# Linear attention and gated FFN on one core: k and v in 128 partitions with a padded tail slot, their loads at mid-group behind the q transpose, more dummy products at the start

## Chip, cores, metric

One core of a Trainium2 chip runs the whole program. The metric is the device time of one execution in microseconds (us). Single runs of one kernel scatter by 1 to 2% here, so medians and ratios over several runs are quoted. Engines are called as the profile calls them: PE is TensorE, DVE is VectorE, ACT is ScalarE, POOL is GpSimd, SP the queue that issues most DMAs.

## The reference

```python
# q, k, v: (8 batches, 8 heads, 576 rows, 64);  x below: 4608 rows of 512
kv  = einsum('bhsd,bhse->bhde', k, v)          # one 64x64 matrix per head
out = einsum('bhsd,bhde->bhse', q, kv)
out = out / sqrt(mean(out*out) + 1e-6) * g_norm
x   = out as (4608, 512)
xn  = x / sqrt(mean(x*x) + 1e-6) * rms_g
y   = (silu(xn @ w_gate) * (xn @ w_val)) @ w_out   # 512 -> 1536 -> 512
```

## The kernel before

The kernel works in nine groups of 512 rows: group n takes the first 512 rows of batch n, and the ninth group takes the 64 rows that are left of each batch. A group is 16 slots of PE work: 12 `up` slots (8 products of 512 columns each, into `g_ps` and `v_ps`) and 4 `down` slots (12 products each, into `o_ps`). Between the slots stand small steps that prepare the next group: k and v are loaded in float32 (`kraw`), cast to bf16 (`k_t`, `v_t`), multiplied to `kv_all`; q is loaded (`stage`), cast (`q_t`) and transposed by a DMA (`qt`); the attention output is scaled (`xna`) and transposed (`xnt`). In the timelines below each engine takes its instructions in program order (a silu stands behind two k casts that wait 1.22 us for their load), so where a step stands decides what waits behind it.

```python
def load_kv_parts(b, name, cuts):              # KP = 96 partitions, KT = 6 tokens each
    src = {"k": k, "v": v}[name][b].rearrange("h (p t) d -> p h (t d)", t=KT)
    st = kraw_pool.tile([KP, H, KT * D], FP32, name="kraw")
    ...
        yield nc.sync.dma_start(out=st[:, hs, :], in_=src[:, hs, :])
# ... (cut)
for n in range(1, B + 1):
    # ... (cut)
        nxt.qT_dma()                           # q of batch n+1, at the start of group n
    # ... (cut)
        if n == 1:                             # batch 3: load at slot 0, casts on POOL
            at(0, lambda: load_kv(3, "k"), lambda: load_kv(3, "v"))
            for i, piece in enumerate(pieces(3, "k", nc.gpsimd) + pieces(3, "v", nc.gpsimd)):
                at(3 + i, piece)
        at(1, lambda n=n: load_q(n + 2))
    if n + 3 < B:                              # k, v of batch n+3 late in the group
        at(11, lambda n=n: load_kv(n + 3, "k"), lambda n=n: load_kv(n + 3, "v"))
        # ... (cut)
    if 2 <= n < B - 2:                         # ... and cast early in the next, on ACT
        todo = pieces(n + 2, "k", nc.scalar)[2:] + pieces(n + 2, "v", nc.scalar)
        for slot, piece in zip((0, 1, 2, 3, 4, 9), todo):
            at(slot, piece)
    if n + 2 < B:
        at(10, kv_batch(n + 2, 0))             # the k/v products
        at(11, kv_batch(n + 2, 1))
```

## Time and profile before

| | before |
|---|---|
| median when the prediction was made | 363.52 us (3 runs, 360.28 to 364.48) |
| span of the profiled run | 358.4 us |
| PE busy | 324.1 us, 90% |
| first FFN product | 26.4 us |

The page's slices come first: 40 equal parts of the span, each digit a busy share in tenths; the PEclk row is the PE clock that the throttle granted.

```profile
PE   6569998999599899799978999799999999999994
...
PEclk9758999999899999999999999999999999999999
```

PE is full except at the start, at slice 11, and once about every four slices. At the start its clock is half. To see the periodic gap, the span is cut at the first FFN product of each group (the boundaries are read from the timeline). The columns are: stretch, length, busy time with count for PE, PEld, DVE, ACT, POOL, then granted clock, DMA share and GB/s. These are groups 1, 2, 4 and 6:

```profile
69.32:109.94 40.62, 36.44 (x207) 18.25 (x208) 22.58 (x45) 14.89 (x27) 12.15 (x16) 0.96 0.74 173
109.94:145.67 35.73, 33.60 (x184) 16.20 (x184) 19.21 (x42) 20.95 (x36) 0.00 (x0) 1.00 0.64 143
181.82:219.57 37.75, 33.60 (x184) 16.23 (x184) 19.21 (x42) 20.94 (x36) 0.00 (x0) 1.00 0.61 142
256.91:289.03 32.12, 32.07 (x161) 14.85 (x161) 18.54 (x40) 13.42 (x24) 0.00 (x0) 1.00 0.26 66
```

Group 6 loads no k and v any more and is PE-bound (32.07 of 32.12). Groups 1 to 5 lose 2 to 4 us each (length minus PE busy). The waits of PE (who waits, for whom, total us, times, longest) say for what:

```profile
PE g_ps L408 <- ACT silu L401: 8.9, 4, 3.4
PE att_ps L231 <- POOL v_t L101: 4.7, 4, 3.8
PE att_ps L275 <- DMA qt<-q_t: 3.5, 4, 1.6
```

Why ACT is late with silu is seen in its timeline at the start of group 2 (start, duration, instruction, and in brackets how long the engine stood idle before it and for what):

```profile
110.14 0.59 ACT L99 COPY o_sb<-o_ps 128x512 f32<-128x512 f32 x1 [2.00 <-PE o_ps L421]
111.95 1.57 ACT L99 CAST k_t<-kraw 96x768 bf16<-96x768 f32 x2 [1.22 <-DMA kraw<-in_k_dram]
113.43 0.59 ACT L401 ACTIVATE silu<-g_ps 128x512 bf16<-128x512 f32 x1
```

Two k casts stand in front of the group's first silu, and their load is still on its way. The queue that issued it, in its own timeline:

```profile
103.82 0.57 SPq L87 DMA_DIRECT2D kraw<-in_k_dram  x1
104.49 0.52 SPq L87 DMA_DIRECT2D kraw<-in_v_dram  x1
105.58 5.54 SPq L433 DMA_DIRECT2D out_dram<-o_sb  x2
111.21 9.16 SPq L258 DMA_TRANSPOSE qt<-q_t  x1
```

The q transpose is issued behind 2.36 MB of k and v and takes 9 us to issue. Over all seven of them, issue to landing:

```profile
DMA to landing us min/median/max: 4.4/11.4/13.5
```

At the start, stretches of PE (length, busy, clock, DMA share, GB/s):

```profile
10.00:13.00 3.00, 0.24 (x2) 1.00 1.09 240
13.00:15.00 2.00, 1.43 (x13) 0.53 1.09 252
15.00:29.00 14.00, 10.92 (x77) 0.50 1.04 374
```

After 2.8 us of idle the clock drops to half and stays there. While k and v come, the DMA engines are full (a share above 1: the records of their packets overlap) yet move only 240 GB/s; for the weights after 16 us it is about 380.

### The profile page before, as it was taken

The page shows a single profiled execution, that of the slowest core. Times are in us where ns is not written, and L with a number is a line of the kernel's source. Part 1 is how long each engine was busy: PE and PEld are TensorE (multiplying, and loading weights), DVE is VectorE, ACT ScalarE, POOL GpSimd, SP SyncE. Part 2 cuts the span into 40 slices and gives each one's busy share as a digit, 9 for nine tenths or more (in the row PEclk, how much of TensorE's full clock was granted, in tenths as well). Part 3 has the DMA queues.
Part 4 walks back from the last instruction along what each step waited for, and adds up shares of the span by engine and source line. Part 5 has one row for each costly group of instructions (what it writes and reads, how often), then busy time and mean ns, then how long its engine had stood idle before and what let it go on. Part 6 is the DMA issues. An engine that isn't in the chain of part 4 may idle for free.

```text
span 358.4 us, 4740 instructions
## 1 busy us (share of the span) xinstructions
PE 324.1 (90%) x1776; PEld 158.7 (44%) x1786; DVE 180.9 (50%) x392; ACT 170.4 (48%) x293; POOL 33.4 (9%) x48
## 2 busy tenths in 40 slices
PE   6569998999599899799978999799999999999994
PEld 2346354455244354345433454345444445444441
DVE  3552655547831396049604880379139625933310
ACT  3484336427136663476436822873346237423321
POOL 0023360543400000000000000020000000000000
PEclk9758999999899999999999999999999999999999
DMA  8999999959559903990399019990530260061013
GB/s 220 273 385 308 223 377 217 243 146 232 136 117 230 269 1 66 228 316 9 62 226 301 29 24 191 279 182 3 164 72 0 53 183 1 0 119 59 0 30 89
DMA packets 62114, 54.31 MB, mean 152 GB/s; under 512 B 34440, under 2 KB 54924, under 8 KB 62092
## 3 DMA queue, kind: packets, MB, share of 16 engines
q1 hardware_dynamic: 57952, 53.48, 60.3%
q0 software_dynamic: 4128, 0.52, 2.3%
q8 instruction: 14, 0.23, 0.3%
q14 instruction: 8, 0.07, 0.1%
q10 hardware_dynamic: 12, 0.00, 0.0%
HBM read 37.75 MB, written 9.44 MB: 132 GB/s over the span
## 4 chain that ended last, share of the span: by engine, by line
PE 54%; DMA 38%; POOL 3%; SPq 2%; issue 1%; ACT 1%; DVE 0%; POOLq 0%
PE o_ps L421 21%; DMA kraw<-in_v_dram 15%; PE g_ps L408 15%; PE v_ps L414 15%; DMA qt<-q_t 14%; DMA stage<-in_moe_w_gate_dram 5%; DMA kraw<-in_k_dram 2%; PE att_ps L275 2%; PE att_ps L231 2%; POOL v_t L101 2%; DMA stage<-in_q_dram 2%; POOL wg_sb L163 1%; ACT o_sb L99 1%; POOL q_t L101 1%; SPq L258 1%
## 5 line engine op out<-in xcount | busy, mean ns | idle before, releaser
L402 DVE TENSOR_TENSOR h_sb<-silu,v_ps 128x512 bf16<-128x512 bf16 x108 | 74.0, 685 | 139.7 <-ACT silu L401 85.7
L408 PE MATMUL g_ps<-xnt,wg_sb 128*128 128x512 bf16 x424 | 109.7, 381 | 9.4 <-ACT silu L401 8.9
L414 PE MATMUL v_ps<-xnt,wv_sb 128*128 128x512 bf16 x424 | 110.1, 380 | 0.4 <-DVE wv_sb L163 0.4
L401 ACT ACTIVATE silu<-g_ps 128x512 bf16<-128x512 f32 x108 | 64.9, 601 | 67.7 <-PE g_ps L408 58.3
L421 PE MATMUL o_ps<-wo_sb,h_sb 128*128 128x512 bf16 x398 | 89.3, 379 | 0.9 <-ACT wo_sb L99 0.3
L414 PEld LDWEIGHTS <-wv_sb 128*128 128x128 bf16 x424 | 41.6, 98 | 52.5 <-DVE wv_sb L163 2.7
L421 PEld LDWEIGHTS <-h_sb 128*128 128x128 bf16 x432 | 41.5, 98 | 49.0 <-issue 1.4
L408 PEld LDWEIGHTS <-wg_sb 128*128 128x128 bf16 x424 | 40.1, 98 | 51.7 <-issue 11.3
L99 ACT COPY o_sb<-o_ps 128x512 f32<-128x512 f32 x33 | 19.3, 586 | 66.3 <-PE o_ps L421 66.3
L281 ACT ACTIVATE sq<-att_ps 128x512 bf16<-128x512 f32 x28 | 16.7, 597 | 16.1 <-PE att_ps L275 13.0
L231 PE MATMUL att_ps<-v_t,k_t 96*128 96x128 bf16 x192 | 15.3, 232 | 7.9 <-POOL v_t L101 4.7
L356 DVE TENSOR_TENSOR xna<-outa,alpha 128x512 bf16<-128x512 bf16 x32 | 20.0, 685 | 0.1
L286 ACT CAST outa<-att_ps 128x512 bf16<-128x512 f32 x32 | 18.6, 580 | 1.8 <-PE att_ps L275 1.8
L296 DVE TENSOR_REDUCE stats<-sq 128x8 f32<-128x512 bf16 x28 | 19.0, 678 | 0.0
L297 DVE TENSOR_REDUCE stats<-wsq 128x8 f32<-128x512 bf16 x28 | 18.9, 675 | 0.0
L231 PEld LDWEIGHTS <-k_t 96*128 96x128 bf16 x192 | 13.3, 103 | 12.7 <-issue 8.6
L99 ACT CAST v_t<-kraw 96x768 bf16<-96x768 f32 (+1 forms) x18 | 15.5, 862 | 6.5 <-DMA kraw<-in_v_dram 6.5
L99 ACT CAST k_t<-kraw 96x768 bf16<-96x768 f32 x16 | 12.8, 824 | 11.8 <-DMA kraw<-in_k_dram 11.8
L131 POOL DMA_DIRECT2D q_t<-in_q_dram x2 | 2.3, 1172 | 137.7 <-DMA qt<-q_t 137.7
L275 PEld LDWEIGHTS <-qt 128*128 128x128 bf16 x128 | 9.9, 104 | 11.1 <-DMA qt<-q_t 5.4
L275 PE MATMUL att_ps<-kv_all,qt 128*128 128x128 bf16 x112 | 10.9, 219 | 3.5 <-DMA qt<-q_t 3.5
L99 ACT CAST q_t<-stage 128x512 bf16<-128x512 f32 (+1 forms) x21 | 12.4, 638 | 3.2 <-DMA stage<-in_q_dram 3.2
(94 smaller groups left out, 167.9 us busy)
## 6 DMA issues: line engine op xcount, KB each, us to landing
stage<-in_q_dram SPq DMA_DIRECT2D x8, 1024.0 KB, 5.9
out_dram<-o_sb SPq DMA_DIRECT2D x16, 512.0 KB, 4.8
kraw<-in_k_dram SPq DMA_DIRECT2D x7, 1152.0 KB, 8.6
kraw<-in_v_dram SPq DMA_DIRECT2D x7, 1152.0 KB, 17.4
stage<-in_moe_w_gate_dram SPq DMA_DIRECT2D x3, 1024.0 KB, 7.5
stage<-in_moe_w_val_dram SPq DMA_DIRECT2D x3, 1024.0 KB, 15.1
stage<-in_moe_w_out_dram SPq DMA_DIRECT2D x3, 1024.0 KB, 15.5
kraw<-in_k_dram SPq DMA_DIRECT2D x2, 576.0 KB, 9.7
```

Of the source, the lines that this page charges most:

```text
L99: engine.copy(out=out, in_=in_)
L231: nc.tensor.matmul(ps[:, j - js[0], :], lhsT=kk[:, c, 2 * j : 2 * j + 2, :], rhs=vv[:, 2 * j : 2 * j + 2, c * D : (c + 1) * D], start=(j = ...
L275: nc.tensor.matmul(ps[:, 2 * j : 2 * j + 2, :], lhsT=a, rhs=b, start=(j == 0 and i == 0), stop=(j == NS - 1 and i == len(terms) - 1),)
L286: nc.scalar.copy(out=outa, in_=ps)
L296: nc.vector.reduce_sum(out=self.ssq[:, c, :], in_=self.sq, axis=AX.X)
L297: nc.vector.reduce_sum(out=self.wssq[:, c, :], in_=wsq, axis=AX.X)
L356: engine.tensor_tensor(out=self.xna[:, c], in0=self.outa[c], in1=self.alpha[:, c, :].to_broadcast([128, H, D]), op=OP.mult,)
L401: nc.scalar.activation(out=silu, in_=g_ps, func=ACT.Silu)
L402: nc.vector.tensor_tensor(out=self.h[:, j, :], in0=silu, in1=v_ps, op=OP.mult)
L408: nc.tensor.matmul(g_ps, lhsT=wg_sb[:, s, j * 128 : (j + 1) * 128], rhs=x[:, :, s, :], start=(s == 0), stop=(s == NS - 1),)
L414: nc.tensor.matmul(v_ps, lhsT=wv_sb[:, s, j * 128 : (j + 1) * 128], rhs=x[:, :, s, :], start=(s == 0), stop=(s == NS - 1),)
L421: nc.tensor.matmul(ps, lhsT=self.h[:, j, c * 128 : (c + 1) * 128], rhs=wo_sb[:, j, :], start=(j == 0), stop=(j == NF - 1),)
```

## The change

The intent has three parts. *Layout*: k and v lie in 128 partitions of 4 tokens like q, and the last 64 tokens go to an extra slot of 64 partitions, whose other half is zeroed once. *Schedule*: k and v of batch n+2 are loaded at slot 5 and cast at slots 12 to 15, where ACT has little to do; the q transpose moves to slot 12 of the group before, behind that group's `xnt` transposes and ahead of the next loads; the k/v products move to slots 1 and 2 of the group that needs them. *Dummies*: products whose result nobody reads fill PE's gaps in the first group.

```diff
+    def load_kv_main(b, name, h0=0, h1=H):
+        ...
+        nc.sync.dma_start(out=raws[b, name][:, h0:h1, 0 : T * D], in_=main_view(...))
+    def load_kv_tail(b, name):
+        nc.sync.dma_start(
+            out=raws[b, name][0:TAIL, :, T * D :],
+            in_={"k": k, "v": v}[name][b, :, MAIN:S, :].rearrange("h r d -> r h d"),
+        )
+    for st in kraw:
+        nc.gpsimd.memset(st[TAIL:128, :, T * D :], 0.0)
-                for c in range(KT):
+                for c in range(T + 1):
 ...
-    warm_pe(4)
+    warm_pe(9)
     Att.kv_of(0, 0)
 ...                       # further warm_pe(4), (4), (2), (3), (12) between the steps
 ...
+            if n == 1:
+                nxt.qT_dma()
 ...
+            else:                          # every batch but the tail
+                at(1, kv_batch(n + 1, 0))
+                at(2, kv_batch(n + 1, 1))
 ...
             at(1, lambda n=n: load_q(n + 2))
+            at(5, lambda n=n: load_kv(n + 2))
+            for slot, piece in zip((3, 4, 9, 10), pieces(n + 2, "q", nc.scalar)):
+                at(slot, piece)
+            for i, piece in enumerate(pieces(n + 2, "k", nc.scalar) + pieces(n + 2, "v", nc.scalar)):
                 at(12 + i // 2, piece)
 ...
+        if n + 2 <= B:
+            at(12, after.qT_dma)
```

More of the change, by code (lines that the diff above doesn't have):

```diff
@@ L41 @@
     HALF_B = B // 2
-    KP = 96
-    KT = S // KP
     NS = d_model // 128
@@ L47 @@
     NB = NF // JB
-    assert TAIL == 64 and B * TAIL == MAIN and 2 * D == 128 and KP * KT == S
+    assert TAIL == 64 and B * TAIL == MAIN and 2 * D == 128
     consts = ctx.enter_context(tc.tile_pool(name="consts", bufs=1))
-    kraw_pool = ctx.enter_context(tc.tile_pool(name="kraw", bufs=3))
     stage_pool = ctx.enter_context(tc.tile_pool(name="stage", bufs=4))
@@ L79, with main_view, load_kv @@
     casts = {}
-    def load_kv_parts(b, name, cuts):
-        src = {"k": k, "v": v}[name][b].rearrange("h (p t) d -> p h (t d)", t=KT)
-        st = kraw_pool.tile([KP, H, KT * D], FP32, name="kraw")
-        raws[b, name] = st
-        for h0, h1 in zip(cuts, cuts[1:]):
-            hs = slice(h0, h1)
-            yield nc.sync.dma_start(out=st[:, hs, :], in_=src[:, hs, :])
-    def load_kv(b, name):
-        list(load_kv_parts(b, name, (0, H)))
+    kraw = []
+    for i in range(3):
+        kraw.append(consts.tile([128, H, (T + 1) * D], FP32, name=f"kraw{i}"))
+    def main_view(x, b, h0=0, h1=H):
+        return x[b, h0:h1, 0:MAIN, :].rearrange("h (p t) d -> p h (t d)", t=T)
+    def load_kv_main(b, name, h0=0, h1=H):
+        if (b, name) not in raws:
+            raws[b, name] = kraw[(2 * b + "kv".index(name)) % 3]
+        nc.sync.dma_start(
+            out=raws[b, name][:, h0:h1, 0 : T * D], in_=main_view({"k": k, "v": v}[name], b, h0, h1)
+        )
+    def load_kv_tail(b, name):
+        nc.sync.dma_start(
+            out=raws[b, name][0:TAIL, :, T * D :],
+            in_={"k": k, "v": v}[name][b, :, MAIN:S, :].rearrange("h r d -> r h d"),
+        )
+    def load_kv(b):
+        for name in "kv":
+            load_kv_main(b, name)
+            load_kv_tail(b, name)
     def load_q(b):
         st = stage_pool.tile([128, H, T * D], FP32, name="stage")
-        nc.sync.dma_start(out=st, in_=q[b, :, 0:MAIN, :].rearrange("h (p t) d -> p h (t d)", t=T))
+        nc.sync.dma_start(out=st, in_=main_view(q, b))
         raws[b, "q"] = st
@@ L107, in round_in @@
             if name == "k":
-                casts[b, name] = qkv_pool.tile([KP, KT, H, D], BF16, name="k_t")
+                casts[b, name] = qkv_pool.tile([128, T + 1, H, D], BF16, name="k_t")
             elif name == "v":
-                casts[b, name] = qkv_pool.tile([KP, H, KT * D], BF16, name="v_t")
+                casts[b, name] = qkv_pool.tile([128, H, (T + 1) * D], BF16, name="v_t")
             else:
@@ L171 @@
     load_q(0)
-    lk, lv = load_kv_parts(0, "k", (0, 4, 8)), load_kv_parts(0, "v", (0, 4, 6, 8))
-    for it in (lk, lv, lk, lv, lv):
-        next(it)
+    load_kv_main(0, "k", 0, 4)
+    load_kv_tail(0, "k")
+    load_kv_main(0, "v", 0, 4)
+    load_kv_tail(0, "v")
+    load_kv_main(0, "k", 4, 8)
+    load_kv_main(0, "v", 4, 8)
     load_w("g", 0)
@@ L203, with warm_pe @@
     nc.vector.tensor_copy(out=ident_f, in_=identity[0:NS, 0:NS])
-    def warm_pe(n):
-        ps = ops_pool.tile([128, 512], FP32, name="o_ps")
+    def warm_pe(n, pool=ops_pool):
+        ps = pool.tile([128, 512], FP32, name=ps_name(pool))
         for i in range(n):
@@ L220, in __init__ @@
             self.outa = []
-            self.xna = xna_pool.tile([128, T, H, D], BF16, name="xna")
-            xnts[n] = xnt_pool.tile([128, T, NS, 128], BF16, name="xnt")
+            self.xna = None
         @staticmethod
@@ L233, in kv_of @@
                         rhs=vv[:, 2 * j : 2 * j + 2, c * D : (c + 1) * D],
-                        start=(j == js[0] and c == 0), stop=(j == js[-1] and c == KT - 1),
+                        start=(j == js[0] and c == 0), stop=(j == js[-1] and c == T),
                     )
@@ L355, in scale @@
         def scale(self, c, engine):
+            if self.xna is None:
+                self.xna = xna_pool.tile([128, T, H, D], BF16, name="xna")
+                xnts[self.n] = xnt_pool.tile([128, T, NS, 128], BF16, name="xnt")
             engine.tensor_tensor(
@@ L510 @@
     round_in(0, "v", nc.vector, 6, 8)
+    warm_pe(4)
     att.oT(0, gps_pool)
     att.oT(1, gps_pool)
+    warm_pe(4)
     Att.kv_of(0, 1)
@@ L515 @@
     att.stat_mm(1)
+    warm_pe(2)
     att.oT(2, vps_pool)
     att.oT(3, vps_pool)
+    warm_pe(3)
     att.stat_mm(2)
@@ L521 @@
         att.o(c, square=False, pool=(ops_pool, gps_pool)[c // 2], keep=True)
+    warm_pe(12, vps_pool)
     round_w12(0, "g", nc.scalar, 0, 2)
@@ L533 @@
         load_w("v", blk)
-    load_kv(1, "k")
-    load_kv(1, "v")
+    load_kv(1)
     load_q(1)
@@ L554 @@
         7: pieces(1, "k", nc.gpsimd) + pieces(1, "v", nc.gpsimd) + pieces(1, "q", nc.gpsimd),
-        8: [lambda: load_kv(2, "k"), lambda: load_kv(2, "v"), lambda: load_q(2)],
+        8: [lambda: load_kv(2), lambda: load_q(2)],
         9: [kv_batch(1, 0), kv_batch(1, 1)],
@@ L585 @@
         run(steps, j)
+    after = Att(2)
     for n in range(1, B + 1):
         ffn = Ffn(n)
-        nxt = Att(n + 1) if n < B else None
+        nxt = after if n < B else None
         steps = {}
@@ L596 @@
             if n == 1:
-                at(2, kv_batch(2, 0), kv_batch(2, 1))
-            nxt.qT_dma()
+                nxt.qT_dma()
             if nxt.tail:
-                at(3, lambda: nxt.q_mask(0))
-                at(4, lambda: nxt.q_mask(1))
+                at(1, lambda: nxt.q_mask(0))
+                at(2, lambda: nxt.q_mask(1))
+            else:
+                at(1, kv_batch(n + 1, 0))
+                at(2, kv_batch(n + 1, 1))
             for c in range(T):
@@ L608 @@
             at(11, lambda: nxt.scale(2, nc.vector), lambda: nxt.scale(3, nc.vector), lambda: nxt.xT_dma(2, 4))
+        if n + 2 <= B:
+            after = Att(n + 2)
         if n + 2 < B:
-            engine = nc.gpsimd if n == 1 else nc.scalar
-            if n == 1:
-                at(0, lambda: load_kv(3, "k"), lambda: load_kv(3, "v"))
-                for i, piece in enumerate(pieces(3, "k", nc.gpsimd) + pieces(3, "v", nc.gpsimd)):
-                    at(3 + i, piece)
             at(1, lambda n=n: load_q(n + 2))
-            for i, piece in enumerate(pieces(n + 2, "q", nc.scalar)):
+            at(5, lambda n=n: load_kv(n + 2))
+            for slot, piece in zip((3, 4, 9, 10), pieces(n + 2, "q", nc.scalar)):
+                at(slot, piece)
+            for i, piece in enumerate(pieces(n + 2, "k", nc.scalar) + pieces(n + 2, "v", nc.scalar)):
                 at(12 + i // 2, piece)
-        if n + 3 < B:
-            at(11, lambda n=n: load_kv(n + 3, "k"), lambda n=n: load_kv(n + 3, "v"))
-            for piece in pieces(n + 3, "k", nc.scalar)[:2]:
-                at(15, piece)
-        if 2 <= n < B - 2:
-            todo = pieces(n + 2, "k", nc.scalar)[2:] + pieces(n + 2, "v", nc.scalar)
-            for slot, piece in zip((0, 1, 2, 3, 4, 9), todo):
-                at(slot, piece)
-        if n + 2 < B:
-            at(10, kv_batch(n + 2, 0))
-            at(11, kv_batch(n + 2, 1))
-        if n == B - 2:
+        if n + 2 == B:
             load_q_tails()
+        if n + 2 <= B:
+            at(12, after.qT_dma)
         for unit in range(NF + T):
```

## The prediction

> What bounds it now. TensorE is busy for 90% of a 358.4 us span (busy table); gain must come from its gaps and slow clock. From the stretch table and the waits:
>
> (a) Start. The clock is 1.00 until 13 us and 0.50 from 14 to 30 us. The last k/v piece of the first group is cast at 16.5 us; the first FFN products start at 26.3. k/v arrive at 238 GB/s (96 partitions, 1536 B runs), whereas the 128-partition q (1 KB runs) and weights (2 KB) come at about 380.
>
> (b) Group 0, 42.6 us, its first 5 us at half clock.
>
> (c) Groups 1 to 5 take 41.1, 35.9, 36.2, 37.7, 37.3 us, groups 6, 7 and tail 32.2, 33.0, 31.1. The waits name why: group 1 waits 4.1 us for GpSimd's v casts, then has 3 us of half clock; groups 2 to 5: g_ps waits 0.5, 2.3, 2.6, 3.4 us for silu, because ScalarE stands behind k/v casts whose loads are still landing; and 1.6, 0.2, 1.5, 0.3 us for the q transpose. That transpose sits behind 2.3 MB of k/v on the queue (issue 9 to 11 us, median landing 11.4; alone 4.4).
>
> What the change does. k/v load at slot 5 in 128 partitions, casts move to slots 12 to 15, where ScalarE is nearly idle, the q transpose runs half a group ahead, k/v products come at slots 1 and 2. I expect the waits of (c) to go: about 17.5 us, plus about 1.3 from group 1's clock and 1.3 from 20 instead of 24 matmuls in each k/v pair. Estimate from the trace: FFN part 31.1 us + 1.1 + 0.9, so 33.1 us for groups 1 to 6, 33 and 31 after: 262.6 us where 284.4 stood. I leave 2 to 4 us for new small stalls.
>
> Start: the tail is 512 runs of 256 B. The Trainium skill ("DMA: Bandwidth & Descriptors", Specifications) puts line rate at 512 B and over; no run here isolates it. The software queue's 4128 small packets took 2.3% of 16 engines, about 32 ns each, so a tail should cost about 1 us, main 2.8: 3.9 us (estimate) against 4.9, so k and v are 2 us earlier. The 34 dummies fill gaps. The Trainium skill ("TensorE: Matmul & The Clock Gate", Part 1) says that idle windows of about 3.4 us throttle the clock to half; this trace agrees (drop at 13 us after 2.8 us of idle). With a warm clock the first FFN products start at about 23.5 us (ScalarE's weight rounding, 5 us, then limits) and run in 3.5 instead of 5 us. Group 0 ends 5 us earlier, at 64.
>
> Sum: 64 + 262.6 + 3 of stalls + 5.1 after the last product = 334 us of span, against 358.4; as the timed median 338 us (before 363.5).
>
> Shown right by: clock near 1.0 from 10 us on; g_ps waits for silu and att_ps for qt under 1 us per group; groups 1 to 6 of 33 to 34 us; transposes landing in about 5 us; k_t/v_t casts in the down stage.
>
> Wrong if: the clock stays low and the dummies delay the chain (+5); 256 B runs are dearer, delaying all starts; casts at slots 12 to 15 delay o_sb or silu at the group's end; transposes and stores collide with q's load, stalling ScalarE at slot 3; zeroing the tails makes early casts wait.

## The result and the profile after

The changed kernel took 340.19 us (median of 4 runs, 337.18 to 340.71) beside 364.0 us before; the ratio is 0.9348, 95% interval 0.9264 to 0.9432. A ratio here is the mean time of one kernel's fast runs over that of the other's of the same rounds, so it is not quite the ratio of the medians. Executions over 1.5% slower than the fastest of the same kernel are left out of the means. The profiled run: span 337.8 us.

The slices of the page, and the stretches of the same groups 1, 2, 4 and 6:

```profile
PE   6989998799999999999999999999999999999994
...
PEclk9999999999999999999999999999999999999999
```

```profile
68.33:102.81 34.48, 33.44 (x179) 15.95 (x180) 19.59 (x43) 18.27 (x33) 0.00 (x0) 1.00 0.65 172
102.81:136.04 33.23, 33.18 (x180) 15.99 (x180) 19.20 (x42) 20.33 (x36) 0.00 (x0) 1.00 0.64 162
169.27:202.50 33.23, 33.18 (x180) 16.01 (x180) 19.20 (x42) 20.33 (x36) 0.00 (x0) 1.00 0.63 169
235.74:268.97 33.23, 33.18 (x181) 16.01 (x180) 19.20 (x42) 14.57 (x26) 0.00 (x0) 1.00 0.25 64
```

From group 2 on every group is PE-bound: 33.18 us busy in 33.23. The waits of PE that are left lie in the start and in groups 0 and 1; in groups 2 to 5 there is none. The largest of group 0, and what is left of the wait for silu:

```profile
PE o_ps L438 <- DVE wo_sb L113: 1.7, 1, 1.7
...
PE v_ps L431 <- DVE wv_sb L173: 0.9, 3, 0.4
PE g_ps L425 <- ACT silu L418: 0.6, 1, 0.6
```

ACT at the end of group 1 and the start of group 2, and the landing of the q transposes:

```profile
100.42 0.58 ACT L109 COPY o_sb<-o_ps 128x512 f32<-128x512 f32 x1 [0.76 <-PE o_ps L438]
100.90 1.35 ACT L109 CAST v_t<-kraw_109 128x640 bf16<-128x640 f32 x2
103.01 0.58 ACT L109 COPY o_sb<-o_ps 128x512 f32<-128x512 f32 x1 [0.76 <-PE o_ps L438]
103.49 1.35 ACT L109 CAST v_t<-kraw_109 128x640 bf16<-128x640 f32 x2
```

```profile
DMA to landing us min/median/max: 4.3/4.4/5.8
```

The casts wait for no load, and the transposes land in 4.4 us. The last two casts run 2 us into group 2, and no wait of PE comes of it. Before and after, group by group (us; worked out as differences of the first FFN products in the timelines):

| | first product | 0 | 1 | 2 | 3 | 4 | 5 | 6 | 7 | tail | span |
|---|---|---|---|---|---|---|---|---|---|---|---|
| before | 26.4 | 43.0 | 40.6 | 35.7 | 36.2 | 37.8 | 37.3 | 32.1 | 33.0 | 31.2 | 358.4 |
| after | 26.4 | 41.9 | 34.5 | 33.2 | 33.2 | 33.2 | 33.2 | 33.2 | 32.9 | 31.2 | 337.8 |

So 20.3 us of the 20.6 lie in groups 1 to 5 (6.1 + 2.5 + 3.0 + 4.6 + 4.1). The start gained nothing and group 0 one microsecond, though the prediction counted on five. Two readings of the start say where it went. PE in the changed kernel at the start, and ACT's cast that the first k/v product needs:

```profile
10.27 4.02 PE L223 MATMUL o_ps<-qt_tail,identity 128*128 128x512 bf16 x9
...
14.08 0.78 PE L245 MATMUL att_ps<-v_t,k_t 128*128 128x128 bf16 x10
```

```profile
10.98 1.26 ACT L109 CAST v_t<-kraw_109 128x1280 bf16<-128x1280 f32 x1 [1.39 <-DMA kraw_109<-in_v_dram]
13.79 0.72 ACT L109 CAST v_t<-kraw_109 128x640 bf16<-128x640 f32 x1 [1.55 <-DMA kraw_109<-in_v_dram]
```

The cast ended at 12.24 us, but nine dummies of 0.43 us each stood in front of the product until 14.08. A warm product of this size takes 0.22 us (in the timeline four start in 0.86 us). So the array ran at half speed until 14 us, although the record of the granted clock says 1.00 there; only after 14 us was it warm. The control e5 (below) is the same kernel, has the same nine dummies in 4.02 us, and its record says 0.50. The two lines, after and then e5 (length, PE busy, clock, DMA share, GB/s):

```profile
10.00:14.00 4.00, 4.00 (x11) 1.00 1.09 342
10.00:14.00 4.00, 4.00 (x11) 0.50 1.11 320
```

The record of the profile after has no entry before 14.18 us, and the view counts such time as full clock.

The loads themselves did come sooner: v's last part landed by 13.79 us, 7.38 us after q (6.41), against 9.91 us before (6.57 to 16.48). For 2.36 MB that is 320 against 238 GB/s. A stretch before, and one after in which only main parts were moved (length, clock, DMA share, GB/s):

```profile
7.00:13.00 6.00, 1.00 1.09 237
10.00:12.50 2.50, 1.00 1.09 326
```

In group 0, DVE and POOL now work at the same time (both timelines, changed kernel):

```profile
59.44 4.62 POOL L111 TENSOR_SCALAR v_t<-kraw_110 128x640 bf16<-128x640 f32 x4 [1.36 <-DMA kraw_110<-in_v_dram]
```

```profile
59.57 2.25 DVE L373 TENSOR_TENSOR xna<-outa,alpha 128x512 bf16<-128x512 bf16 x2
61.74 1.74 DVE L113 CAST wo_sb<-stage 128x2048 bf16<-128x2048 f32 x1
```

Before, the same two scalings took 1.30 us and the cast of `wo` 1.22, because POOL got its data only at 64.6 us and later. Now PE waits 1.7 us for that `wo`.

### The profile page after: what moved, and what is told of

It reads as the page before. It is cut to its first block, busy times and chain, and to the rows that moved or that the text cites. A ratio compares the mean times of both kernels' runs of the same rounds, so it can differ in the third digit from the quotient of the medians.

```text
span 337.8 us, 4759 instructions
## 1 busy us (share of the span) xinstructions
PE 322.6 (95%) x1772; PEld 157.0 (46%) x1784; DVE 182.7 (54%) x392; ACT 172.5 (51%) x301; POOL 29.2 (9%) x43
## 4 chain that ended last, share of the span: by engine, by line
PE 85%; DVE 9%; ACT 2%; DMA 2%; issue 1%; DVEq 0%
PE v_ps L431 25%; PE o_ps L438 25%; PE g_ps L425 25%; PE att_ps L245 3%; PE att_ps L289 2%; PE o_ps L223 2%; DVE h_sb L419 2%; DMA stage<-in_q_dram 2%; DVE xna L373 1%; DVE wv_sb L173 1%; PE att_ps L262 1%; DVE wo_sb L113 1%; DVE stats L311 1%; PE g_ps L438 1%; PE v_ps L408 1%
## 5 line engine op out<-in xcount | busy, mean ns | idle before, releaser
L373 DVE TENSOR_TENSOR xna<-outa,alpha 128x512 bf16<-128x512 bf16 x32 | 21.9, 743 | 0.1
L109 ACT CAST q_t<-stage 128x512 bf16<-128x512 f32 (+1 forms) x21 | 13.4, 637 | 10.9 <-DMA stage<-in_q_dram 10.9
L223 PE MATMUL o_ps<-qt_tail,identity 128*128 128x512 bf16 x31 | 11.7, 534 | 1.4 <-POOL identity masks.py:199 1.4
L245 PEld LDWEIGHTS <-k_t 128*128 128x128 bf16 x160 | 10.3, 98 | 3.9 <-issue 0.6
L309 DVE TENSOR_TENSOR wsq<-sq,gsq_207 128x512 bf16<-128x512 bf16 x28 | 11.8, 420 | 0.0
L245 PE MATMUL att_ps<-v_t,k_t 128*128 128x128 bf16 x160 | 11.4, 220 | 0.0
```

The source lines that it names most:

```text
L109: engine.copy(out=out, in_=in_)
L245: nc.tensor.matmul(ps[:, j - js[0], :], lhsT=kk[:, c, 2 * j : 2 * j + 2, :], rhs=vv[:, 2 * j : 2 * j + 2, c * D : (c + 1) * D], start=(j = ...
L373: engine.tensor_tensor(out=self.xna[:, c], in0=self.outa[c], in1=self.alpha[:, c, :].to_broadcast([128, H, D]), op=OP.mult,)
```

## The experiments

Theory to begin with ("schedule"): the gain comes from where loads, casts and transposes stand. Rivals: "bandwidth" (faster loads) and "clock" (the dummies). The runs came in three calls; the times before in them were 360.38, 361.31 and 361.84 us (medians). Kernels are compared within a call, or by their ratio to before. All runs gave correct results. The diffs are shortened: dots, and calls that are listed on one line, stand for single lines of the kernel.

**e1, layout alone.** The kernel before with the layout, the zeroing and the start loads of the change; `load_kv(b, name)` calls main and tail at the old places.

```diff
-    KP = 96
-    KT = S // KP
+    KT = T + 1
-    casts[b, name] = qkv_pool.tile([KP, KT, H, D], BF16, name="k_t")
+    casts[b, name] = qkv_pool.tile([128, T + 1, H, D], BF16, name="k_t")
+    def load_kv(b, name):
+        load_kv_main(b, name)
+        load_kv_tail(b, name)
```

> The kernel before with the new layout alone (128 partitions of 4 tokens, zero-padded tail slot, start loads split as in the change); old schedule, no extra dummies. Theory 'schedule' (the gain comes from where loads, casts and transposes stand in a group): groups 2 to 5 keep 35 to 37 us each, time 357 to 361 us, about 1% faster. Rival 'bandwidth' (k/v land sooner, so the waits go): 342 to 350 us. Both expect the last k/v cast of the first group about 2 us earlier than 16.5 us, because nothing on TensorE holds it back here.

Measured: 350.39 us (349.18 to 351.8), ratio 0.972 (0.9662 to 0.9779).

**e2, old layout** in the changed kernel (96 partitions, `KP` and `load_kv_parts` put back, schedule and dummies kept).

```diff
-    def load_kv_main(...): ...
-    def load_kv_tail(...): ...
+    def load_kv_parts(b, name, cuts):   # as before, KP = 96
+    def load_kv(b):
+        for name in "kv":
+            list(load_kv_parts(b, name, (0, H)))
```

> The changed kernel with the old layout (96 partitions of 6 tokens), its schedule and dummies kept. Theory 'schedule': groups 2 to 6 at 33.5 us (0.25 us more than 33.2 for the four extra products of each k/v pair), 341 to 345 us. Rival 'bandwidth': the waits for silu and casts return, groups of 35 us and more, 352 us or more.

Measured: 348.4 us (348.25 to 348.88), ratio 0.9667 (0.9606 to 0.9727). Each lies between what the two theories expected, so neither is right alone. The two ratios multiply to 0.940, close to the change's 0.935. The groups tell the shares apart:

| | first product | 0 | 1 | 2 | 3 | 4 | 5 | 6 | 7 | tail | span |
|---|---|---|---|---|---|---|---|---|---|---|---|
| e1 layout alone | 25.2 | 44.7 | 34.2 | 35.3 | 35.2 | 37.5 | 34.9 | 32.1 | 32.9 | 31.2 | 347.9 |
| e2 old layout | 26.3 | 43.7 | 39.4 | 34.2 | 33.5 | 33.5 | 33.5 | 33.8 | 32.9 | 31.2 | 346.6 |

The layout alone brings group 1 from 40.6 to 34.2 us, as far as the whole change; batch 3 is then loaded and cast in time. From groups 2 to 5 it takes off 4 us in all: their waits for `qt` are gone, and their wait for silu stays. The schedule with the old layout brings groups 3 to 5 to 33.5 us, the 33.2 of the change and the four extra products of each k/v pair, but leaves group 1 at 39.4. The remaining PE waits of e1 after group 1, then those of e2 in group 1:

```profile
PE g_ps L424 <- ACT silu L417: 8.2, 4, 2.6
```

```profile
PE g_ps L410 <- ACT silu L403: 4.3, 1, 4.3
```

The second has its reason on the queue of e2: the transpose of batch 2 waits there for POOL's late q cast, and q of batch 3, which ACT wants at slot 3, stands behind it. ACT waits 7.0 us for that q.

```profile
75.16 1.84 SPq L257 DMA_TRANSPOSE qt<-q_t  x1
77.05 1.18 SPq L94 DMA_DIRECT2D stage<-in_q_dram  x1
```

**e3, no extra dummies** in the changed kernel.

```diff
-    warm_pe(9)
+    warm_pe(4)
-    warm_pe(4) ... warm_pe(4) ... warm_pe(2) ... warm_pe(3) ... warm_pe(12, vps_pool)
```

> The changed kernel without its extra dummies (only the 10 and 4 of before). If the warm clock at the start is worth what group 0's first products show (5.05 us before, 3.4 after), the time is 1 to 3 us longer than the change's 340, first FFN products at 25 to 26.5 us, clock 0.5 up to about 30 us. Rival 'clock' (dummies carry much of the gain): 346 us or more. A third possibility: since dummies ran at 0.43 us each and held up the first k/v products by about 1.8 us, removing them costs nothing.

Measured: 339.63 us median of 4; the profiled run: 348.31 us, clock 0.938 over the whole span. The fast three give 0.9419 (0.936 to 0.9478). Rival "clock" falls. Whether the dummies are worth half a per cent or nothing could not be said without a control on the same chip; e11 repeats it with one.

**e4, dummies alone** in the kernel before.

```diff
-    warm_pe(4)
+    warm_pe(9)
     Att.kv_of(0, 0)
+    warm_pe(4), (4), (2), (3), (12, vps_pool) at the places of the change
```

> The kernel before with the dummies alone. Theory 'schedule': 361 to 364 us, within 1% of before; groups 1 to 5 as long as before. Rival 'clock': 355 us or less. The clock should be near 1.0 from 14 us on.

Measured: 360.57 us, ratio 1.0029 (0.9948 to 1.0111). The profile shows groups 0 and 1 as before (43.0 and 40.6 us). With the old loads the dummies gain nothing, although the clock is 1.00 from 14 to 28 us, where it is 0.50 before.

**e5, control**: the changed kernel unedited, in one call with the next three.

> The changed kernel again, unedited, as the yardstick of this call: 337 to 341 us; first FFN products at 26.4 us and group 0 about 42 us if the granted clock starts the same way.

Measured: 338.97 us (335.46 to 340.37), ratio 0.9359 (0.9295 to 0.9424). Its profile: first product 25.8, group 0 42.0, group 1 33.9 us, span 336.7.

**e6, three holds.** A one-column copy on POOL that reads what DVE writes last makes POOL begin later.

```diff
+    def hold_pool(i, src):
+        nc.gpsimd.tensor_copy(out=hold[:, i : i + 1], in_=src)
-        0: [lambda: round_w12(1, "g", nc.gpsimd)],
+        0: [lambda: hold_pool(0, att.xna[:, 3, 7, 63:64]), lambda: round_w12(1, "g", nc.gpsimd)],
-        7: pieces(1, "k", nc.gpsimd) + pieces(1, "v", nc.gpsimd) + ...
+        7: pieces(1, "k", nc.gpsimd) + [lambda: hold_pool(1, wv_sb[:, 3, 1535:1536])] + ...
+        # casts of batch 2 from down step 7, behind hold_pool(2, nxt.xna[:, 3, 7, 63:64])
```

> The changed kernel with three one-column copies on GpSimd that keep its roundings and casts from running beside VectorE's critical work: block 1's rounding waits for the last scaled tile of group 0, the v and q casts of batch 1 for VectorE's rounding of block 2, the casts of batch 2 for the last scaled tile of batch 1. Theory 'collision' (the earlier loads let GpSimd run beside VectorE, which then takes 1.4 to 1.9 times as long per operation): VectorE's scaling 0.65 us each again, wo cast 1.2 us, TensorE's waits for wo and wv gone, group 0 39 to 40 us, time 3 to 4 us below the control. Rival 'start is bound by loads': group 0 stays at 42 us, time as the control.

Measured: 338.27 us (337.25 to 338.82), ratio 0.9359, as the control. But group 0 did become shorter (40.5 us instead of 42.0) and ended 3.2 us earlier, at 64.6 us, since it also began 1.6 us earlier. DVE ran freely:

```profile
57.02 1.29 DVE L373 TENSOR_TENSOR xna<-outa,alpha 128x512 bf16<-128x512 bf16 x2
58.23 1.22 DVE L113 CAST wo_sb<-stage 128x2048 bf16<-128x2048 f32 x1
```

The wait for `wo` is gone. Group 1 gave 1.9 us back, 35.8 instead of 33.9 us: more than group 0's 1.5, less than the 3.2. ACT there:

```profile
77.27 0.62 ACT L109 CAST q_t<-stage 128x512 bf16<-128x512 f32 x1 [4.68 <-DMA stage<-in_q_dram]
```

It is the wait of e2 again: the held q cast delays a transpose, which delays q of batch 3 on the same queue.

**e7, only the third hold.**

> As the run before, with only the third hold (casts of batch 2). Theory 'collision': 1.7 us of wait for wo and some of the slow scaling go, time about 2 us below the control. Rival: as the control; or slower, if the casts of batch 2 now come too late for the k/v products at slots 1 and 2.

Measured: 338.99 us (337.21 to 341.37), ratio 0.9396 (0.9343 to 0.9448). Group 0 took 39.2 us, 2.8 less than the control's, and group 1 35.7 us, 1.8 more. The third hold alone removes the collision in the down part, and alone makes the new wait.

**e8, three holds, no extra dummies.**

> The run with three holds, without the extra dummies. If the dummies are worth something once the collisions are gone: 1.5 to 3 us slower than with them. If what they win in clock they lose by standing in front of the first k/v products: within 1 us.

Measured: 339.51 us, ratio 0.9391 (0.9352 to 0.9431), against 0.9359 with dummies: about 0.3%, not clear of the noise.

**e9, three holds, and q of batch 3 loaded ahead of the transpose of batch 2.**

```diff
             if n == 1:
+                load_q(3)
                 nxt.qT_dma()
-            at(1, lambda n=n: load_q(n + 2))
+            if n > 1:
+                at(1, lambda n=n: load_q(n + 2))
```

> The run with three holds, and q of batch 3 loaded ahead of the q transpose of batch 2. In the run with holds, group 0 ended 3.2 us earlier but group 1 took 35.8 us instead of 33.9, since ScalarE waited 4.7 us at its q cast: that load stood behind a transpose that waited for GpSimd's held-back q cast. Theory: with the load first that wait is gone, group 1 takes 33.5 to 34 us, time 2 us below the run with holds, 3 below the control: 335 to 337 us. Rival (something else in group 1 takes it again): within 1 us of the control.

Measured: 335.57 us (334.64 to 336.32), ratio 0.9295 (0.9255 to 0.9334); the control had 337.95 us and 0.9343. The profile has group 0 at 40.2 and group 1 at 33.2 us, span 333.1. This is the fastest kernel: 7% below before and about half a per cent below the change. The intervals of the two ratios overlap a little, but the six runs of e9 are narrow, and only one of the control's five fast ones lies below their middle. That one, 335.15 us, is as fast as e9, so the half per cent is likely but not clear of the noise. The early start of this profile (first product at 23.9 us) is not the holds' doing: DVE's steps before that product take as long in e5 and e12, and only begin later. In this profile, as in that of e6, the half clock ended sooner (the stretch from 12.1 to 14 us, e9 and then e12, columns as above), and the first k/v product began at 12.4 us (12.6 in e6, 13.1 in e12, 14.2 in e5):

```profile
12.10:14.00 1.90, 1.85 (x16) 1.00 1.08 363
12.10:14.00 1.90, 1.90 (x12) 0.50 1.10 360
```

**e10, transposes at the group's start** as before; loads and casts as changed.

```diff
-            if n == 1:
-                nxt.qT_dma()
+            nxt.qT_dma()
-            at(12, after.qT_dma)
```

(The two masking steps of the tail's q went back to slots 3 and 4.)

> The changed kernel with every q transpose issued at its group's start, as before the change; loads at slot 5 and casts at slots 12 to 15 stay. Theory 'queue' (the transpose was slow only because it stood behind 2.3 MB of k/v): it lands in 4 to 6 us, groups 2 to 6 at 33.2 to 33.7 us, time within 1 us of the control. Rival 'lead' (the half group of lead is needed): groups of 34 us and more, waits of att_ps for qt or of silu behind a late q cast return, time 4 us or more above the control.

Measured: 341.78 us (339.77 to 342.05), ratio 0.9457 (0.9416 to 0.9498), against 0.9343. Landing of the transposes, and ACT at slot 3 of group 2:

```profile
DMA to landing us min/median/max: 5.0/5.2/5.8
```

```profile
112.21 0.62 ACT L109 CAST q_t<-stage 128x512 bf16<-128x512 f32 x1 [3.09 <-DMA stage<-in_q_dram]
```

The transposes are fast, as theory "queue" said, and nothing waits for `qt`. Yet groups 2 to 5 take 34.2, 34.1, 33.9 and 33.6 us, since now the q load stands behind the transpose and ACT waits for it; PE waits 2.0 us in these groups for silu and for `h_sb`, which silu feeds. So the lead is worth about 3 us (1.0 + 0.9 + 0.7 + 0.4, against the 33.2 us of these groups in the change and in e5). By the trace that is not by having `qt` early but by clearing the queue; no run put the q load ahead of a transpose that stands here, which would prove it. The other 11 us or so of the 14.2 that groups 2 to 5 gained in all need no lead. How they divide between the slots of the loads, the casts and the products, no run separated.

**e11, no extra dummies, again**, and **e12, control**, in one call with e9 and e10.

> The same kernel as the earlier run without the extra dummies, whose profile fell in the slow state; here beside a control on the same chip. If the dummies gain nothing in the changed kernel: within 0.3% of the control. If they gain what the profiles of the first products suggest (1.6 us of FFN products at half clock): 1.5 us or more above it.

> The changed kernel, unedited, as the yardstick of this call: 337 to 341 us.

Measured: e11 340.44 us (340.07 to 342.68), ratio 0.9437 (0.9393 to 0.9481). e12 337.95 us, ratio 0.9343 (0.9291 to 0.9395); its profiled run, 340.22 us, is left out of the ratio. The dummies are worth about 1% in the changed kernel; the two intervals just touch. In e11's profile the clock is half up to 28 us, so the first FFN products, from 25.5 us, begin at half speed; group 0 takes 45.3 us, though this was the longest of e11's runs and some of that may be scatter. PE's waits for DVE in group 0 are as long as with dummies. Where the rest of the 1% lies is open.

## Why the prediction was right or wrong

- *Total.* Predicted 338 us, measured 340.19. The sum was 64 (end of group 0) + 265.6 (groups and their stalls) + 5.1; the trace has 68.3 + 264.8 + 4.7. So the span was missed by 3.8 us (334 against 337.8), nearly all of it before the end of group 0. The median was missed by 2.2 only, by luck: the prediction added 4 us from span to median, and the profiled run took 2.3 (337.8 to 340.08).
- *The waits of groups 1 to 5 go.* Right in size. No wait of PE for silu or `qt` is left in groups 2 to 5, groups 2 to 6 take 33.2 us where 33.1 was estimated, and group 1 34.5. The text credited the schedule with all of it. The runs divide it: groups 2 to 5 follow the schedule (e2), group 1 the layout (short in e1, long in e2). Group 1 of e2 waits for silu behind a late q, and e9 removed such a wait by moving one load forward; whether that would do for group 1 with the old layout, no run tried.
- *The transposes were slow because of their place on the queue.* Right: 4.4 us after the change, and 5.2 us at the old place without k and v before them (e10).
- *k and v come about 2 us sooner.* Right: 2.5 us from q's landing to v's last part. The estimate of 3.9 us for each of k and v was near the 3.7 (half of 7.38), but by two errors that cancel. In the packet records of the trace the two tails took 1.16 us of all 16 DMA engines, so 0.6 us each and not 1; that leaves 3.1 us of the 3.7 for a main part, and not 2.8, since it moved at 326 and not 380 GB/s. The Trainium skill's "DMA: Bandwidth & Descriptors" (Specifications) says that runs below 512 B miss line rate; the trace agrees: a packet of 256 B took 18 ns (median), one of 1 KB 52 ns, which is 14 against 20 bytes per ns.
- *The failed step: "With a warm clock the first FFN products start at about 23.5 us ... Group 0 ends 5 us earlier, at 64."* Measured 26.4 and 68.3 us, one microsecond earlier than before. Two things stood in its place. First, the dummies did not find a warm clock: nine of them took 0.43 us each and held the first k/v product 1.8 us beyond its data. Second, the earlier loads let POOL cast beside DVE, whose scaling then took 1.13 us instead of 0.65; removing that overlap shortened group 0 by 1.5 (e6) to 2.8 us (e7). That the collision cost PE time in group 0 is shown: the wait for `wo` stands also in e1 (1.9 us), which has the new loads alone, and not in e2 and e4, which have the old ones. How much the late k/v product cost was only read from traces, as no run removed it alone. The profiles of e6 and e9, where the half clock ended sooner, have their first FFN product at 24.1 and 23.9 us, near the predicted 23.5; those of e5 and e12, with the same code up to there but for a hold on POOL, at 25.8 and 25.7. By this the clock's part is near 2 us. No edit of e6 or e9 stands in the chain of steps before that product, so which start a run gets looks like chance.
- *Dummies.* Counted on, but not separated, in the prediction. They are worth about 1% with the change (e11 against e12, intervals just touching), about 0.3% with holds, not clear of the noise (e8 against e6), nothing before (e4). The prediction's "this trace agrees" is rough: the clock fell after 2.8 us of idle, less than the about 3.4 that it quotes.

Two pages of the Trainium skill bear on the two things that went wrong. "SBUF — State Buffer" (Who interferes with whom) says that a DVE instruction with two SBUF inputs contends with a GpSimd instruction that reads SBUF, and one with at most one SBUF input outside the two-port modes does not. The trace agrees on both: `xna<-outa,alpha`, with both inputs in SBUF, went from 0.65 to 1.13 us, while `xna<-o_ps,alpha`, with one input in PSUM, kept its 0.65 us beside POOL's rounding at 23.6 us. The cast of `wo` has one input in SBUF and still went from 1.22 to 1.74 us; by the same rule it would have run in a two-port mode, which no view shows. "TensorE: Matmul & The Clock Gate" (Part 1) says that the activity window is free-running and does not reset when a kernel starts. The same 16 transposes at 7 us, with nothing changed ahead of them, took 1.89 us in the profile of e5 and 1.07 in that of e6, and the controls' runs scatter from 335.15 to 340.37 us, which fits; that the scatter comes from this alone was not shown.

## What to carry to other kernels

Ask of an instruction not only when its data can come but what stands behind it on its in-order engine or queue: the casts in front of silu, and the loads in front of a transpose, cost more than their own time, and so did the transpose in front of a load. When loads are made faster, look for work that they release early on an engine that shares something with the critical one; here a one-column copy that held POOL back, with one load moved forward, was worth about half a per cent, not clear of the noise. A dummy product in front of real work on an in-order engine costs its own time too, and here twice as much because the clock was not yet warm (0.43 instead of 0.22 us each).

## What the Trainium skill lacked or had wrong

- "DMA: Bandwidth & Descriptors" gives 512 B as the length from which transfers run at line rate. Here runs of 1536 B in 96 partitions moved 238 GB/s with the DMA engines full, while runs of 1 KB in 128 partitions (main parts of k and v after) moved 326 and the weights (runs of 2 KB, 128 partitions) about 380. In the packet records one of 1536 B took 111 ns (median, 6.5 to 14 us, before), one of 1 KB 52 ns, one of 2 KB 87 ns. So it is not that the runs were short. Whether the 96 partitions are to blame or the length of 1536 B itself, no run separated; no page has a rate for either.
- "TensorE: Matmul & The Clock Gate" warns that clock events in traces can be unreliable. A case to add: in the profile after, the granted clock reads 1.00 from 10 to 14 us while 512-column products take 0.43 us, twice their warm 0.22; in e5 it reads 0.50 for the same dummies. At the start of this trace the durations were right and the record, which begins at 14.18 us, was not.
- "SBUF — State Buffer" describes the shared port as an exclusive lock and quotes single slowdowns. That both engines slow down when each has several instructions in a row is not there with a number: here four POOL casts took 4.62 instead of 2.80 us and two DVE scalings beside them 2.25 instead of 1.29, 1.65 and 1.74 times as long. Nothing here contradicts the page.
